# h of the last two batches as seven block products over both, behind all of the attention

## The chip, the cores and the metric

One core of a Trainium2 chip runs the whole program. The metric is the device time of one execution in microseconds. Five engines work side by side and wait for one another by semaphores: TensorE (PE, with its weight loads PEld), VectorE (DVE), ScalarE (ACT), GpSimd (POOL) and SyncE (SP, here a queue of transfers). Each engine takes its instructions strictly in the order in which the program lists them.

## The reference

Sigmoid attention over 8 batches, 12 heads, 448 positions, 64 values a head, and behind it a SiLU layer over all 3584 tokens:

```python
scores = scale * np.matmul(q, k.transpose(0, 1, 3, 2)) - np.log(S)
attn = 1.0 / (1.0 + np.exp(-scores))
attn_out = np.matmul(attn, v)
x = attn_out.transpose(0, 2, 1, 3).reshape(B * S, H * D)   # 3584 x 768
h = x @ w_in                                               # 768 x 2048
g = h * (1.0 / (1.0 + np.exp(-h)))
out = g @ w_out                                            # 2048 x 768
```

## The kernel before

All weights stay in SBUF as f16, w_in as 6 chunks of 128 rows (`w_in_sb`), w_out as 16 (`w_out_sb`). The order of every engine's work is written out by hand (`manual_schedule`).

**Attention** goes by g, a group of four heads of one batch: three for a batch, 24 in all. A unit (g, ch) is one of seven score tiles of a group. `scores` issues four matmuls of 64 x 64 for it, whose result stands in two PSUM banks, and a Sigmoid on ScalarE (L207) into `attnT`. A unit uses a pair of banks of the pool `ps_sc` (two pairs, 4 banks); the first unit of a burst of three takes two single banks of the pool `ps_1` (4 banks) instead, with two Sigmoids. The Sigmoid of the third unit of a burst is put off (L180) until other work of ScalarE's has been issued. `values` (L218) multiplies the seven tiles of a group by v in two single banks (`pav`); two scalings on VectorE (L243) write them into `xT` of the batch, and this releases the next loads.

**h** of a batch is 16 units (`h_unit`, L255), each 6 matmuls of 448 columns into one single bank `ph` (L262), a Sigmoid on ScalarE (`tsig`, L274) and a product on VectorE (L276) into `gTr`. `gTr` holds two batches side by side: 16 blocks of 128 features by 896 tokens.

**The output** goes by sets (`out_set`, L319) of two blocks of 128 tokens: seven products of 8 matmuls of 384 columns (`po`, L338; Strassen's scheme in Winograd's form), with four sums of gTr on VectorE (`S`, lines 350 to 360), eight scaled adds into `osb` (L346) and one copy `m1` on ScalarE (L353). A pair of batches m has three sets; its seventh token block is kept (`kept`, L412) until the next pair has one too, and the two make a fourth set. Four sums of w_out are made once (`w_sums`).

**Order.** `all_moe` is a generator that yields after each matmul of h and output: h of batch 2m, for m > 0 the first set, h of batch 2m + 1, the other sets. The main loop takes bursts of two or three score units (`burst`), the values of a group that is complete, the rows of a later one (copied on VectorE, transposed by a DMA on SP's queue, `dma_transpose`), and then a stretch of that stream (`stretch`), as long as the pace of the batch says. Loads of q, k and v are issued on GpSimd's queue, three or four groups ahead.

Of the kernel before, what the change touches and what calls it, by code (L numbers as in the profile page):

```python
# [17 lines left out]
def kernel(  # L18
# [9 lines left out]
    nc = tc.nc  # L28
# [116 lines left out]
    def pe_transpose(g, pieces=(("k", 0, 4), ("k", 4, NCH), ("q", 0, 4), ("q", 4, NCH))):  # L145
        if ("k", g) not in qkT:
            new_qkT(g)
        for name, c0, c1, *copy in pieces:
# [12 lines left out]
                dst[:, c0 * P : c1 * P], ptr[:, : (c1 - c0) * P]  # L161
            )

    def dma_transpose(g, name, copy):
        if ("k", g) not in qkT:
            new_qkT(g)
        rows = p3.tile([P, NCH, 2, D], F16, tag=f"{name}r", name=f"{name}r")
        copy(rows, flat[name, g].rearrange("p j c d -> p c j d"))  # L168
        nc.sync.dma_start_transpose(
            out=qkT[name, g], in_=rows.rearrange("p c j d -> p (c j d)")  # L170
        )

    attnT = {}

    late = []

# [5 lines left out]
    def scores(g, ch, banks=None, put_off=False):  # L182


        attnT[g, ch] = p12.tile([P, 2, S], F16, tag="attnT", name="attnT")
        if banks is None:
            psc = ps_sc.tile([P, 2, 512], F32, tag="pssc", name="psc")
            banks = [psc[:, j] for j in range(2)]
            parts = [(attnT[g, ch], psc[:, :, :S])]
        else:  # L190
            parts = [(attnT[g, ch][:, j], banks[j][:, :S]) for j in range(2)]
        for half in range(2):
            own = slice(half * HP, (half + 1) * HP)
            for j in range(2):
                rows = slice(j * D, (j + 1) * D)
                nc.tensor.matmul(  # L196
                    banks[j][own, :S],
                    qkT["k", g][rows, ch, own],
                    qkT["q", g][rows, :, own],
                    start=True,  # L200
                    stop=True,
                )
        if put_off:
            late.extend(parts)
            return
        for to, psc in parts:
            nc.scalar.activation(to, psc, AF.Sigmoid, bias=bias_s, scale=QKSCALE)  # L207
# [10 lines left out]
    def values(g, end=NCH):  # L218
        b, iq = divmod(g, NQ)
        if b not in xT:  # L220
            assert b < 2 or b - 2 in h_done
            xT[b] = p2.tile([P, NPAIR, S], F16, tag="xT", name="xT")
        pav, done_rounds = part_of.pop(g, None) or (
            [ps_1.tile([P, 512], F32, tag="ps1", name="pav") for _ in range(2)],
            0,
        )
        for ch in range(done_rounds, end):
            at = attnT.pop((g, ch))
            for half in range(2):
                own = slice(half * HP, (half + 1) * HP)  # L230
                for j in range(2):
                    nc.tensor.matmul(  # L232
                        pav[half][j * D : (j + 1) * D, :S],
                        flat["v", g][own, j, ch, :],
                        at[own, j, :],
                        start=(ch == 0),
                        stop=(ch == NCH - 1),
                    )
        if end < NCH:
            part_of[g] = pav, end  # L240
            return
        for half in range(2):
            nc.vector.tensor_scalar_mul(xT[b][:, half * NQ + iq, :], pav[half][:, :S], SX)  # L243
        if iq == NQ - 1:
            ready.add(b)

# [69 lines left out]
    def row_blocks(m, g):  # L316
        return [rows_of[2 * m + u // NCH, u % NCH] for u in (2 * g, 2 * g + 1)]

    def out_set(a1, rows1, a2, rows2, last=False):  # L319
        nonlocal hold, weight  # L320
        weight = SET_WEIGHT
        lo, hi = slice(0, NHC), slice(NHC, NFC)
        osb = [p4.tile([P, DMODEL], F32, tag="osb", name="osb") for _ in range(2)]
        c11, c12 = (osb[0][:, nh * NO2 : (nh + 1) * NO2] for nh in range(2))
        c21, c22 = (osb[1][:, nh * NO2 : (nh + 1) * NO2] for nh in range(2))
        m1 = p2.tile([P, NO2], F32, tag="m1", name="m1")
        sg = [cpool.tile([P, NHC, P], F16, tag=f"S{i}", name=f"S{i}") for i in range(1, 5)]

        def store(rows, o, cols, engines):
            for at, (row, eng) in enumerate(zip(rows, engines)):  # L330
                eng.dma_start(row[:, cols], o[at * HP : (at + 1) * HP, cols])

        left, right, whole = slice(0, NO2), slice(NO2, DMODEL), slice(0, DMODEL)

        def product(a, w):
            po = ps_1.tile([P, 512], F32, tag="ps1", name="po")
            for fc in range(NHC):
                nc.tensor.matmul(  # L338
                    po[:, :NO2], a[:, fc, :], w[:, fc, :], start=(fc == 0), stop=(fc == NHC - 1)
                )  # L340
                if fc < NHC - 1:
                    yield 163
            return po[:, :NO2]

        def plus(o, po, x, sign=ISX):
            nc.vector.scalar_tensor_tensor(  # L346
                out=o, in0=po, scalar=sign, in1=x, op0=ALU.mult, op1=ALU.add
            )

        nc.vector.tensor_sub(sg[2], a1[:, lo], a2[:, lo])  # L350
        nc.vector.tensor_add(sg[0], a2[:, lo], a2[:, hi])
        po = yield from product(a1[:, lo], wq[0][0])
        nc.scalar.activation(m1, po, AF.Copy, scale=ISX)  # L353
        late_sigmoid()
        nc.vector.tensor_sub(sg[1], sg[0], a1[:, lo])
        hold = False
        yield 163
        po = yield from product(a1[:, hi], wq[1][0])
        plus(c11, po, m1)
        nc.vector.tensor_sub(sg[3], a1[:, hi], sg[1])  # L360
        if last:
            store(rows1, osb[0], left, (nc.sync, nc.sync))
        yield 163
        po = yield from product(sg[2], tw[3])
        plus(c22, po, m1)
        yield 163
        po = yield from product(sg[1], tw[2])
        plus(c22, po, c22)
        plus(c12, po, m1)
        yield 163  # L370
        po = yield from product(a2[:, hi], tw[4])
        plus(c21, po, c22, -ISX)
# [12 lines left out]
        yield 163  # L385


    by_h1 = {3: 6, 6: 7, 9: 8}
    early = [h_unit(0, fc) for fc in range(2)]
    sums = w_sums()  # L390

    def moe_h(b):
        for fc in range(NFC):
            yield from early[fc] if b == 0 and fc < 2 else h_unit(b, fc)
            if b == 1:
                if fc >= 2:
                    next(sums)
                if fc in by_h1:
                    for name in ("k", "q"):
                        dma_transpose(by_h1[fc], name, act_copy)  # L400
                    if by_h1[fc] == 8:

                        nc.gpsimd.tensor_copy(gate, qkT["q", 8][:1, 0, :1])
                        for to in (10, 11, 12):
                            load("kq", to)

    def moe_set(m, g):
        step = out_set(block(g), row_blocks(m, g), block(g + 1), row_blocks(m, g + 1))
        for i, ns in enumerate(step):
            if m % 2 == 0 and g == 2 and i % 8 == 4 and i < 32:  # L410
                fcs = slice(i // 8 * 4, i // 8 * 4 + 4)
                nc.scalar.activation(kept[:, fcs], block(NCH - 1)[:, fcs], AF.Copy)  # L412
            if m == 0 and g == 0 and i in (10, 14):
                next(sums)
            if m == 0 and g == 0 and i in (24, 40):
                dma_transpose(9, "k" if i == 24 else "q", nc.vector.tensor_copy)
                if i == 40:
                    load("kq", 13)
            yield ns

    def all_moe():
        for m in range(B // 2):
            yield from moe_h(2 * m)
            if m > 0:
                yield from moe_set(m, 0)
            yield from moe_h(2 * m + 1)
            if m == 0:
                yield from moe_set(m, 0)
            yield from moe_set(m, 2)
            yield from moe_set(m, 4)  # L430
            if m % 2 == 1:
                g = NCH - 1
                yield from out_set(
                    kept, row_blocks(m - 1, g), block(g), row_blocks(m, g), m == B // 2 - 1
                )

    later = []
# [144 lines left out]
            do(*what)  # L582

    TILES = {2: 3, 3: 2, 4: 3, 5: 3, 6: 3, 7: 3}
    paces = {1: 1600, 2: 2400, 3: 2500, 4: 3400, 5: 3200, 6: 3000, 7: 2800}
    def burst(n, tiles):

        new = units[n : n + (tiles if not waiting else 2)]
# [56 lines left out]
```

## Time and profile before

| | us |
|---|---|
| median of 3 runs | 378.05 (377.73 to 378.10) |
| the profiled execution | 377.84 |
| its span, first to last instruction | 376.0 |
| TensorE busy in the span | 367.9 |
| last score matmul begins a burst at | 317.99 |
| h of batch 7, 96 matmuls in a row | 326.42 to 344.58 |
| last 168 output matmuls | 344.58 to 371.9 |

| stretch, us | PE | DVE | ACT | POOL | DMA share |
|---|---|---|---|---|---|
| 29 to 52 | 22.19 | 11.56 | 19.36 | 11.63 | 1.27 |
| 52 to 152 | 99.99 | 70.23 | 72.28 | 21.77 | 1.09 |
| 152 to 322 | 169.93 | 103.93 | 116.54 | 12.81 | 0.53 |
| 326 to 345 | 19.00 | 10.28 | 8.54 | 0.00 | 0.15 |
| 345 to 376 | 26.88 | 20.76 | 1.64 | 0.00 | 0.29 |

A share of busy time is an average over stages that differ. Matmuls are pipelined and the profile models their ends, so a busy TensorE need not be at its peak. The granted clock is 1.00 throughout. In the list of groups, each line has the line of the kernel, the engine, what is written and read, how often, the busy time and the mean of one, and the idle time ahead of it with the engine that ended it.

### The profile page before, as it was taken

To read this page: it belongs to the slowest core of one execution; us is meant where nothing else is said; L and a number is where in the kernel's file an instruction comes from. 1 tells how busy PE (TensorE), PEld (TensorE's weight loads), DVE (VectorE), ACT (ScalarE), POOL (GpSimd) and SP (SyncE) were. 2 spreads that over 40 slices of the span, in tenths; PEclk is the share of its full clock that TensorE was granted. 3 is DMA by queue.
4 is the path that set the end of the run, shared out by engine and by line. 5 is a ranking of instruction groups with operands and counts; after the bars stand their busy time and mean duration, and the time that the engine had idled before them with its cause. 6 is when DMAs were issued, how large, how long until landed. Compare 5 with 4: busy or idle time off the path is not lost.

```text
span 376.0 us, 7623 instructions
## 1 busy us (share of the span) xinstructions
PE 367.9 (98%) x3081; PEld 189.2 (50%) x3081; DVE 233.9 (62%) x417; ACT 243.2 (65%) x355; POOL 66.1 (18%) x99
## 2 busy tenths in 40 slices
PE   7999999999999999999999999999999999999995
PEld 3554445555554455455555545544555445555663
DVE  2664447997666466548676547645675457556773
ACT  5998886778766866676557676677866685243000
POOL 8566432053211002102120200000010000000000
PEclk9999999999999999999999999999999999999999
DMA  8999999959999909909499834546072300200333
GB/s 131 200 204 201 205 203 204 180 89 142 215 178 182 217 2 111 189 32 118 71 160 161 145 92 75 51 108 75 0 149 36 85 2 2 54 30 2 83 86 84
DMA packets 65698, 42.79 MB, mean 114 GB/s; under 512 B 36096, under 2 KB 62208, under 8 KB 65664
## 3 DMA queue, kind: packets, MB, share of 16 engines
q0 software_dynamic: 27072, 22.58, 42.5%
q1 hardware_dynamic: 38240, 19.44, 29.0%
q8 instruction: 24, 0.39, 0.4%
q10 hardware_dynamic: 352, 0.30, 0.2%
q14 instruction: 10, 0.08, 0.1%
HBM read 45.61 MB, written 11.01 MB: 151 GB/s over the span
## 4 chain that ended last, share of the span: by engine, by line
PE 91%; DMA 3%; ACT 2%; POOL 2%; issue 1%; DVE 0%; POOLq 0%; ACTq 0%
PE ph L262 38%; PE po L338 34%; PE psc L196 9%; PE pav L232 8%; DMA qf<-in_q_dram 3%; ACT attnT L207 1%; POOL kf L82 1%; POOL vf L82 1%; PE ptrq L153 0%; POOL qf L82 0%; ACT tsig L274 0%; DVE gTr L276 0%; ACT attnT L180 0%; PE ptrk L153 0%; DVE osb L346 0%
## 5 line engine op out<-in xcount | busy, mean ns | idle before, releaser
L207 ACT ACTIVATE attnT<-psc,bias_s 128x896 f16<-128x896 f32 (+1 forms) x168 | 138.5, 894 | 45.1 <-PE psc L196 44.9
L262 PE MATMUL ph<-xT,w_in_sb 128*128 128x448 f16 x768 | 151.2, 353 | 0.0
L276 DVE TENSOR_TENSOR gTr<-ph,tsig 128x448 f16<-128x448 f32 x128 | 78.3, 623 | 71.4 <-ACT tsig L274 70.9
L262 PEld LDWEIGHTS <-w_in_sb 128*128 128x128 f16 x768 | 72.8, 98 | 74.0 <-issue 9.2
L274 ACT ACTIVATE tsig<-ph 128x448 f16<-128x448 f32 x128 | 68.3, 549 | 49.1 <-PE ph L262 48.2
L338 PEld LDWEIGHTS <-S 128*128 128x128 f16 x448 | 42.3, 98 | 33.5 <-issue 7.2
L346 DVE SCALAR_TENSOR_TENSOR osb<-po,osb 128x384 f32<-128x384 f32 x70 | 37.6, 554 | 22.2 <-PE po L338 21.9
L196 PE MATMUL psc<-qT,kT 64*64 64x448 f16 x672 | 49.1, 360 | 1.5 <-ACT qT L143 0.5
L243 DVE TENSOR_SCALAR xT<-pav 128x448 f16<-128x448 f32 x48 | 27.7, 620 | 28.9 <-PE pav L232 28.9
L82 POOL DMA_DIRECT2D vf<-in_v_dram x24 | 17.2, 718 | 161.0 <-PE pav L232 138.6
L338 PE MATMUL po<-T,S 128*128 128x384 f16 x224 | 40.6, 327 | 0.0
L338 PEld LDWEIGHTS <-gTr 128*128 128x128 f16 x304 | 28.7, 98 | 23.5 <-issue 5.4
L338 PE MATMUL po<-w_out_sb,S 128*128 128x384 f16 x224 | 39.9, 326 | 0.0
L232 PE MATMUL pav<-attnT,vf 64*64 64x448 f16 x672 | 38.1, 350 | 0.4 <-DVE gTr L276 0.4
L338 PE MATMUL po<-w_out_sb,gTr 128*128 128x384 f16 x192 | 34.9, 327 | 0.0
L196 PEld LDWEIGHTS <-kT 64*64 64x64 f16 x672 | 16.4, 105 | 28.3 <-issue 23.1
L232 PEld LDWEIGHTS <-vf 64*64 64x64 f16 x672 | 20.9, 107 | 12.6 <-issue 2.7
L346 DVE SCALAR_TENSOR_TENSOR osb<-po,m 128x384 f32<-128x384 f32 x42 | 23.2, 553 | 6.3 <-PE po L338 5.1
L180 ACT ACTIVATE attnT<-psc,bias_s 128x896 f16<-128x896 f32 x26 | 26.6, 1022 | 0.0
L353 ACT ACTIVATE m<-po 128x384 f32<-128x384 f32 x14 | 6.9, 495 | 23.7 <-PE po L338 23.7
L338 PE MATMUL po<-T,gTr 128*128 128x384 f16 x112 | 21.4, 326 | 0.0
L82 POOL DMA_DIRECT2D kf<-in_k_dram x25 | 18.0, 721 | 18.0 <-DVE kr L168 9.6
(43 smaller groups left out, 153.6 us busy)
## 6 DMA issues: line engine op xcount, KB each, us to landing
out_dram<-osb SPq DMA_DIRECT2D x54, 192.0 KB, 3.2
vf<-in_v_dram POOLq DMA_DIRECT2D x24, 224.0 KB, 6.1
kf<-in_k_dram POOLq DMA_DIRECT2D x23, 224.0 KB, 7.9
qf<-in_q_dram POOLq DMA_DIRECT2D x23, 224.0 KB, 8.1
w_in_sb<-in_moe_w_in_dram POOLq DMA_DIRECT2D x16, 192.0 KB, 8.3
w_out_sb<-in_moe_w_out_dram POOLq DMA_DIRECT2D x4, 768.0 KB, 15.7
kT<-kr SPq DMA_TRANSPOSE x18, 7.3
qT<-qr SPq DMA_TRANSPOSE x18, 6.7
```

Source lines behind the costliest of these rows:

```text
L82: nc.gpsimd.dma_start(flat[name, g][:, :, c0:c1].rearrange("p i c d -> p i (c d)"), rows_in(name, g)[:, :, c0 * D : c1 * D],)
L180: nc.scalar.activation(to, psc, AF.Sigmoid, bias=bias_s, scale=QKSCALE)
L196: nc.tensor.matmul(banks[j][own, :S], qkT["k", g][rows, ch, own], qkT["q", g][rows, :, own], start=True, stop=True,)
L207: nc.scalar.activation(to, psc, AF.Sigmoid, bias=bias_s, scale=QKSCALE)
L232: nc.tensor.matmul(pav[half][j * D : (j + 1) * D, :S], flat["v", g][own, j, ch, :], at[own, j, :], start=(ch == 0), stop=(ch == NCH - 1),)
L243: nc.vector.tensor_scalar_mul(xT[b][:, half * NQ + iq, :], pav[half][:, :S], SX)
L262: nc.tensor.matmul(ph[:, :S], w_in_sb[:, cc, fc * P : (fc + 1) * P], xT[b][:, cc, :], start=(at == 0), stop=(at == NCC - 1),)
L274: nc.scalar.activation(tsig, ph[:, :S], AF.Sigmoid, bias=0.0, scale=ISX)
L276: nc.vector.tensor_mul(gTr[:, fc, (b % 2) * S : (b % 2) * S + S], ph[:, :S], tsig)
L338: nc.tensor.matmul(po[:, :NO2], a[:, fc, :], w[:, fc, :], start=(fc == 0), stop=(fc == NHC - 1))
L346: nc.vector.scalar_tensor_tensor(out=o, in0=po, scalar=sign, in1=x, op0=ALU.mult, op1=ALU.add)
L353: nc.scalar.activation(m1, po, AF.Copy, scale=ISX)
```

## The change

For the last two batches (6, "even", and 7, "odd") h is no longer made batch by batch. w_in is cut into four quadrants (two halves of the features by two halves of the 768 inputs), the two batches' xT into four blocks, and seven products replace eight. `h_pair` goes by f, the 8 pairs of feature blocks f and f + 8. For each f it makes seven products of 3 matmuls: `first(f)` makes products one and two, `group(f)` makes six, seven and five, three and four. Products one, two and six take single banks; seven and five share one pair of `ps_sc` banks, three and four the other. `first(0)` and `first(1)` run ahead of groups 0 and 1; from f = 2 on, `first(f)` runs just ahead of `group(f)`.

The seven results are combined by adds on VectorE into f32 tiles `mid` (in the buffers of `attnT`), by copies on ScalarE and ten adds on GpSimd; SiLU is then one function on ScalarE (`AF.Silu`) straight into `gTr`, in place of the Sigmoid and the product on VectorE. The scale 1/64 goes into it, so the last sets use a scale of 1 (`scale_of`), and the kept block is rescaled when it is copied.

Sums of the operands are made ahead: 16 of w_in (four kinds for each quarter t, one kind in place, the others in buffers of the attention that are free by then; `next_w_in_sum`, called in the h of batch 5 and in the sets of m = 2), and 12 of xT (`x_sums`, four behind the values of each group of batch 7). The first set of m = 2 moves behind the h of batch 5. The paces of batches 4 to 7 go from 3400, 3200, 3000, 2800 to 2800, 2500, 2350, 2300, so that the score units end while the sets of m = 2 still run.

The core of the diff:

```diff
@@ values @@
+        if b == B - 1:
+            x_sums(iq)
@@ out_set @@
-    def out_set(a1, rows1, a2, rows2, last=False):
+    def out_set(a1, rows1, a2, rows2, scale=ISX, last=False):
-        nc.scalar.activation(m1, po, AF.Copy, scale=ISX)
+        nc.scalar.activation(m1, po, AF.Copy, scale=scale)
+    def w_in_sum(i, t):
+        a11, a12, a21, a22 = (w_in_part(r, c, t) for r in range(2) for c in range(2))
...
+        if i == 1:
+            nc.vector.tensor_add(a21, a21, a22)
+        elif i == 2:
+            nc.vector.tensor_sub(ws[2, t], a21, a11)
+        elif i == 3:
+            nc.vector.tensor_sub(ws[3, t], a11, a21)
+        else:
+            nc.vector.tensor_sub(ws[4, t], a12, ws[2, t])
+    def x_sums(iq):
...
+        b11, b12, b21, b22 = even[:, iq], odd[:, iq], even[:, NH + iq], odd[:, NH + iq]
+        nc.vector.tensor_sub(xs[1, iq], b12, b11)
+        nc.vector.tensor_sub(b12, b22, b12)
+        nc.vector.tensor_sub(xs[2, iq], b22, xs[1, iq])
+        nc.vector.tensor_sub(xs[4, iq], b21, xs[2, iq])
+        xs[3, iq] = b12
+    def h_pair():
...
+        def silu(fc, b, h):
+            nc.scalar.activation(
+                gTr[:, fc, b % 2 * S : (b % 2 + 1) * S], h, AF.Silu, bias=0.0, scale=ISX
+            )
...
+        def first(f):
+            one, m1, c11 = single(), middle(), middle()
+            yield from product(one, f, quadrant(0, 0), x_part(0, even))
+            act_copy(m1, one)
+            while put_off:
+                silu(*put_off.pop(0))
+            yield 189
+            two = single()
+            yield from product(two, f, quadrant(0, 1), x_part(1, even))
+            nc.vector.tensor_add(c11, two, m1)
+            silu(f, even, c11)
+            yield 189
+            return m1
+        def group(f, m1):
+            u2, u3, u4, c22, c21 = (middle() for _ in range(5))
+            six = single()
+            yield from product(six, f, w_sum(2), x_sum(2))
+            nc.vector.tensor_add(u2, six, m1)
+            yield 189
+            seven, five = pair()
+            yield from product(seven, f, w_sum(3), x_sum(3))
+            yield 189
+            yield from product(five, f, w_sum(1), x_sum(1))
+            nc.vector.tensor_add(u3, seven, u2)
+            nc.vector.tensor_add(c22, five, u3)
+            nc.vector.tensor_add(u4, five, u2)
+            silu(NHC + f, odd, c22)
+            yield 189
+            three, four = pair()
+            yield from product(three, f, w_sum(4), x_part(1, odd))
+            yield 189
+            yield from product(four, f, quadrant(1, 1), x_sum(4))
+            if f == NHC - 1:
+                nc.vector.tensor_add(c21, four, u3)
+                silu(NHC + f, even, c21)
+                nc.vector.tensor_add(u4, three, u4)
+                silu(f, odd, u4)
+            else:
+                act_copy(c21, four)
+                if f % 2 == 0:
+                    nc.vector.tensor_add(u4, three, u4)
+                else:
+                    act_copy(u2, three)
+                nc.gpsimd.tensor_add(c21, c21, u3)
+                if f % 2 == 1:
+                    nc.gpsimd.tensor_add(u4, u2, u4)
+                put_off.extend(((f, odd, u4), (NHC + f, even, c21))[:: 1 if f % 2 == 0 else -1])
+            yield 189
@@ moe_h, moe_set @@
+            if b == B - 3:
+                units_done = fc + 1
+                next_w_in_sum()
...
+            if m == B // 2 - 2 and i % 8 == 4:
+                next_w_in_sum()
@@ all_moe @@
-            yield from moe_h(2 * m)
-            if m > 0:
-                yield from moe_set(m, 0)
-            yield from moe_h(2 * m + 1)
-            if m == 0:
+            if m == B // 2 - 1:
+                yield from h_pair()
+            else:
+                yield from moe_h(2 * m)
+                if m == 1:
+                    yield from moe_set(m, 0)
+                yield from moe_h(2 * m + 1)
+            if m != 1:
                 yield from moe_set(m, 0)
@@ paces @@
-    paces = {1: 1600, 2: 2400, 3: 2500, 4: 3400, 5: 3200, 6: 3000, 7: 2800}
+    paces = {1: 1600, 2: 2400, 3: 2500, 4: 2800, 5: 2500, 6: 2350, 7: 2300}
```

More of the change, by code (lines that the diff above doesn't have):

```diff
@@ L162, in pe_transpose @@
             )
+    in_rows = set()
     def dma_transpose(g, name, copy):
@@ L166, in dma_transpose @@
             new_qkT(g)
+        in_rows.add((name, g))
         rows = p3.tile([P, NCH, 2, D], F16, tag=f"{name}r", name=f"{name}r")
@@ L173 @@
     attnT = {}
+    scored = 0
     late = []
@@ L182, in scores @@
     def scores(g, ch, banks=None, put_off=False):
+        nonlocal scored
+        scored = g + (ch == NCH - 1)
         attnT[g, ch] = p12.tile([P, 2, S], F16, tag="attnT", name="attnT")
@@ L343, in product, with plus @@
             return po[:, :NO2]
-        def plus(o, po, x, sign=ISX):
+        def plus(o, po, x, sign=scale):
             nc.vector.scalar_tensor_tensor(
@@ L371, in out_set @@
         po = yield from product(a2[:, hi], tw[4])
-        plus(c21, po, c22, -ISX)
+        plus(c21, po, c22, -scale)
         yield 163
@@ L385, in out_set, with w_in_part @@
         yield 163
+    NH = NCC // 2
+    ws = {}
+    def w_in_part(r, c, t):
+        at = r * DFF // 2 + 2 * t * P
+        return w_in_sb[:, c * NH : (c + 1) * NH, at : at + 2 * P]
+    def w_in_sum(i, t):
+        a11, a12, a21, a22 = (w_in_part(r, c, t) for r in range(2) for c in range(2))
+        if i == 1:
+            ws[1, t] = a21
+        elif i == 4:
+            kT = p4.tile([P, NCH, P], F16, tag="kT", name="w4")
+            ws[4, t] = kT.rearrange("p c t -> p (c t)")
+        else:
+            tag = "kf" if i == 3 else "qf"
+            f = p4.tile([P, 2, NCH, D], F16, tag=tag, name=f"w{i}")
+            ws[i, t] = f.rearrange("p i c d -> p (i c d)")
+        if i > 1:
+            ws[i, t] = ws[i, t][:, : NH * 2 * P].rearrange("p (c f) -> p c f", c=NH)
+        if i == 1:
+            nc.vector.tensor_add(a21, a21, a22)
[5 more added lines that the diff above has]
+            nc.vector.tensor_sub(ws[4, t], a12, ws[2, t])
@@ new lines, with next_w_in_sum @@
+    w_in_sums = [(i, t) for t in range(4) for i in (3, 1, 2, 4)]
+    units_done = 0
+    def next_w_in_sum():
+        blocked = set()
+        for i, t in w_in_sums:
+            g = NQB - 4 + t
+            if (
+                units_done > NHC + 2 * t + 1
+                if i == 1
+                else scored > g
+                if i == 4
+                else ("k" if i == 3 else "q", g) in in_rows
+            ) and t not in blocked:
+                w_in_sums.remove((i, t))
+                w_in_sum(i, t)
+                return
+            blocked.add(t)
@@ new lines @@
+    xs = {}
+    def x_sums(iq):
+        even, odd = xT[B - 2], xT[B - 1]
+        if not xs:
+            rows = [
+                p3.tile([P, NCH, 2, D], F16, tag=f"{name}r", name=f"x{name}").rearrange(
+                    "p c j d -> p (c j d)"
+                )
+                for name in "kkkqq"
+            ]
+            for i, (at, end) in {
+                1: (rows[0], rows[1][:, :S]),
+                2: (rows[2], rows[1][:, S:]),
+                4: (rows[3], rows[4][:, :S]),
+            }.items():
+                for c in range(NH):
+                    xs[i, c] = at[:, c * S : (c + 1) * S] if c < 2 else end
+        b11, b12, b21, b22 = even[:, iq], odd[:, iq], even[:, NH + iq], odd[:, NH + iq]
[4 more added lines that the diff above has]
+        xs[3, iq] = b12
@@ new lines, in h_pair, with middle, product, quadrant @@
+    def h_pair():
+        even, odd = B - 2, B - 1
+        put_off = []
+        def middle():
+            return p12.tile([P, S], F32, tag="attnT", name="mid")
+        def product(o, f, a, x):
+            for c in range(NH):
+                nc.tensor.matmul(o, a(f, c), x(c), start=(c == 0), stop=(c == NH - 1))
+                if c < NH - 1:
+                    yield 189
+        def quadrant(r, c):
+            at = r * DFF // 2
+            return lambda f, i: w_in_sb[:, c * NH + i, at + f * P : at + (f + 1) * P]
+        def w_sum(i):
+            return lambda f, c: ws[i, f // 2][:, c, f % 2 * P : (f % 2 + 1) * P]
+        def x_part(r, b):
+            return lambda c: xT[b][:, r * NH + c, :]
+        def x_sum(i):
+            return lambda c: xs[i, c]
+        def silu(fc, b, h):
+            nc.scalar.activation(
+                gTr[:, fc, b % 2 * S : (b % 2 + 1) * S], h, AF.Silu, bias=0.0, scale=ISX
+            )
+        def single():
+            return ps_1.tile([P, 512], F32, tag="ps1", name="ph")[:, :S]
+        def pair():
+            both = ps_sc.tile([P, 2, 512], F32, tag="pssc", name="ph2")
+            return both[:, 0, :S], both[:, 1, :S]
+        def first(f):
+            assert even in ready and not w_in_sums
+            one, m1, c11 = single(), middle(), middle()
[11 more added lines that the diff above has]
+        def group(f, m1):
+            assert odd in ready
+            u2, u3, u4, c22, c21 = (middle() for _ in range(5))
[31 more added lines that the diff above has]
+                put_off.extend(((f, odd, u4), (NHC + f, even, c21))[:: 1 if f % 2 == 0 else -1])
+            yield 189
+        m1s = []
+        for f in range(2):
+            m1s.append((yield from first(f)))
+        for f in range(NHC):
+            m1 = m1s[f] if f < 2 else (yield from first(f))
+            yield from group(f, m1)
+        h_done.update((even, odd))
@@ L392, in moe_h @@
     def moe_h(b):
+        nonlocal units_done
         for fc in range(NFC):
             yield from early[fc] if b == 0 and fc < 2 else h_unit(b, fc)
+            if b == B - 3:
+                units_done = fc + 1
+                next_w_in_sum()
             if b == 1:
@@ L405, in moe_h, with scale_of @@
                             load("kq", to)
+    def scale_of(m):
+        return 1.0 if m == B // 2 - 1 else ISX
     def moe_set(m, g):
-        step = out_set(block(g), row_blocks(m, g), block(g + 1), row_blocks(m, g + 1))
+        step = out_set(
+            block(g), row_blocks(m, g), block(g + 1), row_blocks(m, g + 1), scale_of(m)
+        )
         for i, ns in enumerate(step):
@@ L411, in moe_set @@
                 fcs = slice(i // 8 * 4, i // 8 * 4 + 4)
-                nc.scalar.activation(kept[:, fcs], block(NCH - 1)[:, fcs], AF.Copy)
+                nc.scalar.activation(
+                    kept[:, fcs],
+                    block(NCH - 1)[:, fcs],
+                    AF.Copy,
+                    scale=scale_of(m) / scale_of(m + 1),
+                )
+            if m == B // 2 - 2 and i % 8 == 4:
+                next_w_in_sum()
             if m == 0 and g == 0 and i in (10, 14):
@@ L422, in all_moe @@
         for m in range(B // 2):
-            yield from moe_h(2 * m)
-            if m > 0:
-                yield from moe_set(m, 0)
-            yield from moe_h(2 * m + 1)
-            if m == 0:
+            if m == B // 2 - 1:
+                yield from h_pair()
+            else:
+                yield from moe_h(2 * m)
[3 more added lines that the diff above has]
+            if m != 1:
                 yield from moe_set(m, 0)
@@ L433, in all_moe @@
                 yield from out_set(
-                    kept, row_blocks(m - 1, g), block(g), row_blocks(m, g), m == B // 2 - 1
+                    kept,
+                    row_blocks(m - 1, g),
+                    block(g),
+                    row_blocks(m, g),
+                    scale_of(m),
+                    m == B // 2 - 1,
                 )
```

## The prediction

> **What bounds the kernel now.** I read the page's busy shares first, then the busy times by stretch, then the chain that ended last, then the timeline at the end.
>
> ```profile
> PE 367.9 (98%) x3081; PEld 189.2 (50%) x3081; DVE 233.9 (62%) x417; ACT 243.2 (65%) x355; POOL 66.1 (18%) x99
> ...
> PE 91%; DMA 3%; ACT 2%; POOL 2%; issue 1%; DVE 0%; POOLq 0%; ACTq 0%
> PE ph L262 38%; PE po L338 34%; PE psc L196 9%; PE pav L232 8%; DMA qf<-in_q_dram 3%; ACT attnT L207 1%; POOL kf L82 1%; POOL vf L82 1%; PE ptrq L153 0%; POOL qf L82 0%; ACT tsig L274 0%; DVE gTr L276 0%; ACT attnT L180 0%; PE ptrk L153 0%; DVE osb L346 0%
> ```
> ```profile
> 152.00:322.00 170.00, 169.93 (x1385) 87.35 (x1381) 103.93 (x183) 116.54 (x177) 12.81 (x18) 1.00 0.53 84
> ...
> 326.00:345.00 19.00, 19.00 (x103) 9.91 (x102) 10.28 (x17) 8.54 (x16) 0.00 (x0) 1.00 0.15 42
> ```
>
> The columns of the second fence are PE, PEld, DVE, ACT and POOL busy, the granted clock, the DMA share and GB/s. TensorE is the chain for 91% of the span, at full clock. A busy PE in this profile need not be PE at its peak, so I checked with counts. The chain gives the price of each kind: 96 matmuls of h in 18.16 us (0.189 each), 168 of the output in 27.31 (0.163 each), 28 of the values in 1.32, three units of scores in 0.69 (0.23 each). From 152 to 318, counts times these prices leave only 0.10 to 0.16 us per burst of scores, but for one place:
>
> ```profile
> 267.13 0.49 ACT m L353
> 267.62 1.95 ACT attnT L207 x3
> 269.57 0.52 ACT kept L412
> 270.09 0.91 ACT attnT L180
> 271.00 0.04 issue
> 271.04 0.38 PE psc L196 x4
> ```
>
> Here the second score unit of a burst waits for the bank pair that the put-off sigmoid of the burst before (L180) still reads; it costs about 0.4 us. The reader is to see that a burst of three units keeps ScalarE for at least 0.4 + 1.95 + 0.95 = 3.3 us, so a burst must be followed by that much TensorE work.
>
> **The change, part by part.**
>
> *Fewer matmuls.* h of batches 6 and 7 is 2 x 16 x 6 = 192 matmuls; seven products of 3 for each of 8 pairs of blocks are 168. The order of the built program shows 744 matmuls of h in place of 768. 24 x 0.189 = **-4.54 us**. Nothing else leaves TensorE.
>
> *All attention earlier.* From unit 84 on, the stretches between bursts hold 288 matmuls of h and 303 of the output in place of 384 and 370: TensorE's work there falls from 167.2 to 138.2 us by the prices above. ScalarE's, at 1.0 us a unit, 0.55 per h unit (L274) and 0.5 per m (L353), falls from about 121 to 112, so its share goes from 73% to 81%. In the h of batch 5 a burst of three is followed by 26 matmuls: TensorE 0.7 + 4.9 + 0.1 = 5.7, ScalarE 3.1 + 4.33 x 0.52 = 5.4. It fits, and the next burst, with values, has slack (ScalarE 3.5 of 5.1). Of the output sets of m = 2, the tightest bursts have 13 and 16 matmuls behind them. With 13 the next burst begins at 2.9 and its second unit at 3.15, while the put-off sigmoid ends at 3.3 to 3.4: 0.25. With 16 after a burst that had a kept copy (0.65) ahead of its put-off sigmoid, the shift passes on and the second unit waits about 0.5. Together 0 to 1.2; I take **+0.5**.
>
> *Sums on VectorE.* 16 of w_in (128 x 768 f16: L308's row, 0.549) are 8.8 us; 12 of x (448 f16) go by the slope between 768 (0.549) and 1024 (0.685) elements to 0.38 each, 1.6 us per group of four since each needs the one before. VectorE had 103.9 busy of 170; less 16 gTr (0.62) and 1.2 sets (7.2 each), plus 8.8 and two x groups, it has about 97 of 140. Idle time covers them, and the score bursts wait on the xT scalings, which stand ahead of the x sums. Where cover is gone is the last pav: its second bank waits for c11 of the set's second product. From the end of the pav before, VectorE has two xT (1.2), four x sums (1.6), one osb (0.5), three S (1.9), a w_in sum (0.5) and c11 (0.55): 6.3. TensorE has 11 + 17 output matmuls and a burst: 1.8 + 0.8 + 2.8 = 5.4. I take **+0.8** (0 to 1.1). The third x group is covered by the 31 output matmuls and two `first` units behind it (5.0 + 2.3 us against 2.8).
>
> *Banks of h.* Each group's first pair (products seven and five) is freed by u3, c22 and u4 on VectorE. In steady state five more products (2.83 us) pass before it is wanted again; three adds at 0.62 (L276's row, same size out of PSUM) need about 2.0. Between groups 0 and 1 only three products (1.70) pass, and the Silu table load stands in ScalarE's queue between the two m1 copies. The only load in the trace took 1.28 us (L481). With h starting at 0: m1 of block 0 is copied by 1.3, the load ends at 2.55, Silu of c11 at 3.1, the second m1 copy at 3.55, then VectorE's c11 4.2, u2 4.75, u3 5.4, c22 6.05, u4 6.6. The pair is wanted at 5.67: **+0.9** (0 without the load's delay, 1.0).
>
> The Trainium skill ("ScalarE: Activation LUTs", Terms) puts a table load at about 2.7 us; the trace has 1.28 and decides. By the page the last term would be an estimated 2.4 and the sum 1.4 higher.
>
> *Per pair of groups* TensorE has 42 x 0.189 = 7.94, ScalarE 13 operations at a pitch of about 0.47 to 0.5 (6.3), VectorE 11 adds (6.4): all fit. But one circle runs through two engines: m1 copy, then c11, u2, u3, c22 (2.5, the dependent ones at full length), Silu of c22 (0.59), copies of c21 and the next m1 (0.93) = 4.0, and 4.5 in an odd group with u2's copy: 8.5 against 7.94. The excess of 0.54 per two groups is first taken from slack; walking it on, seven waits 0.3 at group 5 and 0.5 at group 7. Bounds 0 and 1.6 (three times 0.54): **+0.4**.
>
> *End of h.* The first output set's second product needs Silu of the last c21. With ScalarE idle that is 0.2 + 0.62 + 0.04 + 0.55 + 0.05 = 1.46 after the last h matmul, against 8 x 0.163 = 1.30 of the first product: 0.16. With the circle's lateness (Silu of c22 ends 1.75 after the last h matmul, then c21's) it is 1.55. Between: **+0.9**. Before, this seam had none: the h of batch 7 ran into a set whose blocks it finished early.
>
> *GpSimd* gets 10 adds of 448 f32. No two-input operation of it is in the trace. Memsets of 128 x 1 and 128 x 128 (0.096, 0.224) give 1.0 ns an element, the affine select (one read, 0.289) 1.5; two reads at 0.5 each make 2.0 ns, 0.1 + 0.9 = 1.0 us. Bounds 0.62 (VectorE's add) and 2.0 (twice). At 1.0 it sets nothing. Its loads and SP's transposes keep their places: loads land after 6 to 8 us and are used three and four heads later, over 30 us even now. SP's stores of the last sets only stand later, with 27 us of output behind the first.
>
> **Sum** against the profiled execution: 376.0 - 4.54 + 0.5 + 0.8 + 0.9 + 0.4 + 0.9 = 375.0 of span. Its own time was 377.84 (1.84 around the span) and the median is 378.05, 0.2 more. So 375.0 + 1.84 + 0.2 = **377.0 us**, 1.0 less than before.
>
> **Rivals.**
>
> 1. *All cover holds* (fast): the five stalls at their low bounds, 0 + 0 + 0 + 0 + 0.16, give 378.05 - 4.4 = 373.7. For it: TensorE had no idle in 170 us of like bursts. Against: the wait at 271 shows such seams cost something when work behind a burst is short.
> 2. *GpSimd's adds set the end* (slower): in odd groups two adds follow one another and ScalarE's queue waits for the second. Copy of c21, two adds, three Silus, copies, adds and Silu of the next group make 6.0 + 2g for an add of g, against 7.94; from g = 1.24 it overtakes the 8.5 circle. At g = 1.5, 9.0 - 7.94 = 1.06 three times is 3.2 in place of 0.4, and the end seam grows to 1.3: 377.0 + 2.8 + 0.4 = 380.2. Against: the slope above.
> 3. *The first GpSimd add alone is long*. The group-1 adds queue behind it; each us beyond about 3.5 delays ScalarE, and so the pair, by one. From 5.3 the change is slower; at 6, 377.0 + 2.5 = 379.5. Against: the first memset and select in the trace show no such gap. The Trainium skill ("GPSIMD Engine Reference", 2.1 Instruction dispatch) says that the first call to a freshly loaded kernel pays some 6 us that show as no instruction; no run here yet shows it for an add.
> 4. *Attention becomes ScalarE's* (slower): bursts at 5.4 of 5.7 us leave 0.3. If the order of Sigmoids and bank waits eats it, six such bursts at 0.4 are 2.4, and the sets go to 1.2: 377.0 + 2.4 + 0.7 = 380.1. Against: bursts at 89% (297 to 304) ran without a stall.
>
> **How the numbers follow.** Forecast 0.45 (own range 375.9 to 378.2), rival 1 0.17, 2 0.15, 3 0.08, 4 0.15. About 0.2%, 0.76 us, is what can be told from no change, so faster means below 377.3. Two thirds of the forecast's chance lies there, with all of rival 1: 0.47. Slower (above 378.8) are rivals 2 to 4 but for a sliver: 0.37. The rest, 0.16, is the same. The range leaves out the fast half of rival 1 and the slow ends of 2 to 4: **374.3 to 380.4**.
>
> **What would show it.** 744 h matmuls; the stretch of 168 last ones longer than 31.8 us by about 1.3; product seven of group 1 waiting on u4; the last pav waiting on VectorE near 0.8; the second product of the first last set waiting on a Silu; score units waiting on L184's Sigmoid in the sets of m = 2. Wrong it would be if waits of TensorE add up to over 5 us or under 2, or if GpSimd's add is over 1.24.

## The result

The change makes the kernel a little slower: 379.58 us (379.01 to 379.91, 6 runs) against 378.08 (377.72 to 378.42, 6 runs), a ratio of 1.0038 (95% interval 1.0025 to 1.0051). The forecast was 377.0, faster by 1.0; the time fell inside the range of 374.3 to 380.4, on the other side of no change.

The profiled execution took 379.65, its span 377.9. First the busy shares and the chain of waits on the page of the changed kernel:

```profile
PE 366.9 (97%) x3057; PEld 188.1 (50%) x3057; DVE 251.7 (67%) x459; ACT 251.9 (67%) x374; POOL 77.3 (20%) x109
...
PE 80%; ACT 8%; DVE 8%; issue 3%; DVEq 0%; ACTq 0%
```

TensorE has 24 matmuls fewer, which at 0.189 each are 4.54 us, yet its busy time falls by only 1.0, and it is the chain for only 80% of the span where it was 91%: 8% each now run through ScalarE and VectorE. Next the list of what TensorE waited for (total, times, longest); the lines left out stand in the list of the kernel before as well:

```profile
PE ph L483 <- DVE mid L543: 1.7, 3, 1.0
...
PE po L346 <- ACT gTr L501: 0.4, 1, 0.4
...
PE pav L238 <- DVE osb L354: 0.3, 1, 0.3
PE psc L202 <- ACT attnT L184: 0.2, 1, 0.2
PE po L346 <- DVE S L358: 0.2, 1, 0.2
```

L483 is the line of all the new products, L543 the add that makes u4. These lines show where to look, not how much is lost: short waits are not listed, and the busy time that fell by 1.0 in place of 4.54 shows that some of the loss counts as busy. So I measured stage by stage, as length less count times price (0.189, 0.163, 1.32 and 0.23, as in the prediction). The busy times by stretch (PE, PEld, DVE, ACT and POOL busy, granted clock, DMA share, GB/s) of the attention, of the seven products and of what follows them:

```profile
152.00:291.00 139.00, 138.79 (x1201) 70.47 (x1197) 91.51 (x169) 104.04 (x156) 12.84 (x18) 1.00 0.57 95
301.50:336.20 34.70, 32.92 (x170) 16.39 (x169) 24.53 (x44) 24.43 (x48) 11.24 (x10) 1.00 0.09 23
```

In the second stretch TensorE is idle for 1.8 of 34.7 us, at a granted clock of 1.00.

| what TensorE lost or gained, us | predicted | measured | from |
|---|---|---|---|
| 24 fewer matmuls of h | -4.54 | -4.54 | 744 h matmuls (576 and 168) |
| attention closer together | +0.5 | +1.13 | excess over counts from the burst at 147.27 to the last one at 290.79: 5.32; before, from 146.55 to 317.99: 4.19 |
| last value product | +0.8 | +0.87 | its end at 296.44; by counts 295.57 |
| bank pair of groups 0 and 1 | +0.9 | +1.18 | from product six to seven of group 1: 306.59 to 308.34, by counts 0.57 |
| circle of ScalarE and VectorE | +0.4 | +1.71 | the seven of groups 2 to 7 come 4.06, 4.13, 4.22, 4.48, 4.15 and 4.49 after those of the group before, by counts 3.97 |
| end of h | +0.9 | +0.91 | from the last product of h to product three of the set: 336.17 to 339.68, by counts 2.60 |
| sum | -1.04 | +1.26 | |

The row of the last value product is its whole excess over the counts. The same instructions of the kernel before, from its last burst at 317.99 to 323.49, have 0.23 of it already, so 0.64 is new and the sum by that is 1.03.

The spans of the two profiled executions differ by 1.9. The first score burst of batch 2 began at 77.54 before and at 78.27 after, though both kernels list the same work up to there; 1.9 less that 0.73 is 1.17, close to both sums.

The bank pair, in the timeline of the changed kernel (start, length, engine, line, operation, in brackets the idle time and what ended it):

```profile
302.31 0.54 ACT L143 ACTIVATE mid<-ph 128x448 f32<-128x448 f32 x1 [8.08 <-PE ph L483]
302.88 1.28 ACT L501 ACT_TABLE_LOAD   x1
...
304.17 0.58 ACT L501 ACTIVATE gTr<-mid 128x448 f16<-128x448 f32 x1
...
304.65 0.52 ACT L143 ACTIVATE mid<-ph 128x448 f32<-128x448 f32 x1
...
306.59 0.73 PE L483 MATMUL ph<-xk,w 128*128 128x448 f16 x3
...
307.67 0.61 DVE L543 TENSOR_TENSOR mid<-ph,mid 128x448 f32<-128x448 f32 x1
...
308.34 0.73 PE L483 MATMUL ph<-xT,w 128*128 128x448 f16 x3 [1.01 <-DVE mid L543]
```

The table load stands between the two copies of m1, as walked in the prediction, and product seven of group 1 starts within 0.06 us of the end of u4. The Trainium skill ("ScalarE: Activation LUTs", Terms) has about 2.7 us for a load; here it took 1.28 and the Silu behind it began at once, so the trace differs and decides.

The circle, one turn of two groups:

```profile
325.17 0.96 ACT L143 ACTIVATE mid<-ph 128x448 f32<-128x448 f32 x2
325.23 0.73 PE L483 MATMUL ph<-xT,w 128*128 128x448 f16 x3 [0.35 <-DVE mid L543]
...
326.26 0.61 DVE L523 TENSOR_TENSOR mid<-ph,mid 128x448 f32<-128x448 f32 x1
...
328.18 0.62 DVE L542 TENSOR_TENSOR mid<-ph,mid 128x448 f32<-128x448 f32 x1
...
328.83 0.58 ACT L501 ACTIVATE gTr<-mid 128x448 f16<-128x448 f32 x1 [0.85 <-DVE mid L542]
329.32 1.39 ACT L143 ACTIVATE mid<-ph 128x448 f32<-128x448 f32 x3
...
333.80 0.96 ACT L143 ACTIVATE mid<-ph 128x448 f32<-128x448 f32 x2
333.87 0.73 PE L483 MATMUL ph<-xT,w 128*128 128x448 f16 x3 [0.35 <-DVE mid L543]
```

Read it as a ring: the copies at 325.17 release c11 (L523), a row of dependent adds on VectorE ends in c22 (L542), ScalarE stands idle 0.85 until it can make the Silu of c22, and only behind that Silu, in its queue, come the copies that release the next c11. From 325.17 to 333.80 one turn takes 8.63; TensorE's 42 matmuls need 7.94. GpSimd is not in it, but by a small margin. Its adds took 1.14 (7 and 3 of them), the first 1.13; ScalarE waits for the second of two in a row (Silu at 323.54), and the Silu of c22 two places behind (324.68) then comes only 0.1 later than ScalarE could have begun it.

And the attention, in the chain of waits of the changed kernel, at the output set behind the h of batch 5:

```profile
262.29 0.49 ACT m L361
262.78 1.95 ACT attnT L213 x3
264.73 0.91 ACT attnT L184
265.63 0.04 issue
265.68 0.38 PE psc L202 x4
```

It is the picture that the kernel before had at 269.57 to 271.04: the second score unit of a burst waits for the bank pair that the put-off Sigmoid (L184) still reads. The burst at 184.05, in a set of m = 1, loses as much in another way, as the timeline of VectorE ahead of it shows:

```profile
182.85 0.61 DVE L171 COPY kr<-kf 128x896 f16<-128x896 f16 x1
183.37 0.55 DVE L354 SCALAR_TENSOR_TENSOR osb<-po,osb 128x384 f32<-128x384 f32 x1
183.84 0.55 DVE L354 SCALAR_TENSOR_TENSOR osb<-po,m 128x384 f32<-128x384 f32 x1
```

The second matmul of that burst starts at 184.44, 0.05 after the last of these adds, which frees its single bank; a copy of rows for a transpose (L171) stands ahead of the two adds. ScalarE was idle for 2.67 at this place.

### The profile page after: what moved, and what is told of

It reads as the page before. It is cut to its first block, busy times and chain, and to the rows that moved or that the text cites. A ratio compares the mean times of both kernels' runs of the same rounds, so it can differ in the third digit from the quotient of the medians.

```text
span 377.9 us, 7681 instructions
## 1 busy us (share of the span) xinstructions
PE 366.9 (97%) x3057; PEld 188.1 (50%) x3057; DVE 251.7 (67%) x459; ACT 251.9 (67%) x374; POOL 77.3 (20%) x109
## 4 chain that ended last, share of the span: by engine, by line
PE 80%; ACT 8%; DVE 8%; issue 3%; DVEq 0%; ACTq 0%
PE po L346 32%; PE ph L270 28%; PE psc L202 9%; PE pav L238 8%; ACT attnT L213 5%; ACT mid L143 2%; DVE mid L541 1%; DVE mid L542 1%; DVE mid L535 1%; PE pw L140 1%; DVE mid L523 1%; PE ptrq L153 1%; DVE osb L354 0%; DVE mid L558 0%; ACT tsig L282 0%
## 5 line engine op out<-in xcount | busy, mean ns | idle before, releaser
L270 PE MATMUL ph<-xT,w_in_sb 128*128 128x448 f16 x576 | 114.4, 353 | 0.0
L284 DVE TENSOR_TENSOR gTr<-ph,tsig 128x448 f16<-128x448 f32 x96 | 58.4, 621 | 51.7 <-ACT tsig L282 51.1
L270 PEld LDWEIGHTS <-w_in_sb 128*128 128x128 f16 x576 | 54.1, 98 | 56.5 <-issue 9.0
L282 ACT ACTIVATE tsig<-ph 128x448 f16<-128x448 f32 x96 | 50.7, 551 | 24.7 <-PE ph L270 24.3
L346 PEld LDWEIGHTS <-S 128*128 128x128 f16 x448 | 42.1, 98 | 34.5 <-issue 7.5
L202 PE MATMUL psc<-qT,kT 64*64 64x448 f16 x672 | 49.9, 360 | 1.6 <-ACT attnT L213 0.5
L346 PE MATMUL po<-T,S 128*128 128x384 f16 x224 | 40.6, 327 | 0.2 <-DVE S L358 0.2
L346 PEld LDWEIGHTS <-gTr 128*128 128x128 f16 x304 | 28.7, 98 | 23.4 <-issue 4.5
L346 PE MATMUL po<-w_out_sb,S 128*128 128x384 f16 x224 | 40.3, 327 | 0.0
L346 PE MATMUL po<-w_out_sb,gTr 128*128 128x384 f16 x192 | 34.9, 327 | 0.4 <-ACT gTr L501 0.4
L184 ACT ACTIVATE attnT<-psc,bias_s 128x896 f16<-128x896 f32 x26 | 26.5, 1021 | 0.0
L501 ACT ACTIVATE gTr<-mid 128x448 f16<-128x448 f32 x32 | 17.5, 575 | 10.7 <-DVE mid L542 6.5
```

The source lines that it names most:

```text
L202: nc.tensor.matmul(banks[j][own, :S], qkT["k", g][rows, ch, own], qkT["q", g][rows, :, own], start=True, stop=True,)
L270: nc.tensor.matmul(ph[:, :S], w_in_sb[:, cc, fc * P : (fc + 1) * P], xT[b][:, cc, :], start=(at == 0), stop=(at == NCC - 1),)
L282: nc.scalar.activation(tsig, ph[:, :S], AF.Sigmoid, bias=0.0, scale=ISX)
L284: nc.vector.tensor_mul(gTr[:, fc, (b % 2) * S : (b % 2) * S + S], ph[:, :S], tsig)
L346: nc.tensor.matmul(po[:, :NO2], a[:, fc, :], w[:, fc, :], start=(fc == 0), stop=(fc == NHC - 1))
L501: nc.scalar.activation(gTr[:, fc, b % 2 * S : (b % 2 + 1) * S], h, AF.Silu, bias=0.0, scale=ISX)
```

## The experiments

All are measured against the kernel before on the same chip (its medians were 378.3 to 378.6), so ratios are what compares. The line numbers of an experiment's profile can be a few off those of the changed kernel.

**The Silu of c22 put off** behind the next copy of m1:

```diff
-            silu(NHC + f, odd, c22)
+            if f == NHC - 1:
+                silu(NHC + f, odd, c22)
+            else:
+                put_off.append((NHC + f, odd, c22))
```

> One edit to the changed kernel: the Silu of c22 goes into the put-off list (but for the last group), so ScalarE copies c21 and the next m1 without waiting for VectorE's c22. Theory (the circle m1 copy, c11, u2, u3, c22, Silu, c21 copy, m1 copy runs at 8.6 us per two groups against TensorE's 7.94): the waits of product seven at groups 3 to 7 go, 1.5 to 1.9 us in all; h_pair takes about 32.9 us in place of 34.7, the seam behind it shrinks by some 0.5; time 377.3 to 378.1. Rival (VectorE's adds or the bank pairs themselves are too slow): the waits stay, time within 0.4 of the changed kernel's 379.6. GpSimd as the next limit: waits of ScalarE for its adds grow and half of the gain stays out, 378.6.

377.11 us (376.8 to 377.44), ratio 0.9972 (0.9962 to 0.9982). One Silu of each group (but the last) moved in one queue turns the change from slower to faster. The timeline of this kernel, ScalarE and TensorE at the end of the h:

```profile
328.25 2.08 ACT L501 ACTIVATE gTr<-mid 128x448 f16<-128x448 f32 x4
...
330.31 1.05 ACT L143 ACTIVATE mid<-ph 128x448 f32<-128x448 f32 x2
...
331.75 0.73 PE L483 MATMUL ph<-xT,w 128*128 128x448 f16 x3
...
336.96 2.80 PE L346 MATMUL po<-T,S 128*128 128x384 f16 x16 [0.17 <-DVE S L358]
```

Product seven of the last group (331.75) follows without a wait, ScalarE makes four Silus in one row, and the products take 32.96 us (301.06 to 334.02): 31.78 and the 1.18 of the bank pair. Of the 0.91 at the end of h, 0.3 is left. So the circle is shown, with what its lateness did to the seam.

**The table load ahead**, by a Silu of one column behind the last Sigmoid, in time that ScalarE has to spare:

```diff
+        nc.scalar.activation(warm, bias_s, AF.Silu, bias=0.0, scale=1.0)
         for g in waiting:
             values(g)
```

> One edit to the changed kernel: a one-column Silu right behind the last Sigmoid, so that the table load of 1.28 us falls in 8 us in which ScalarE is idle. Theory (the wait of 1.0 us of product seven in group 1 comes from the load that stands between the two m1 copies): that wait goes to 0.1 or less, time 0.7 to 1.2 lower, 378.4 to 378.9. Rival (only three products pass between the two uses of the pair, and three adds are too slow for that by themselves): the wait stays at 0.5 or more, time 379.2 or above. If the circle takes the gain back, the wait goes but h_pair ends less than 0.5 earlier.

378.87 us, ratio 1.0013 (1.0004 to 1.0022). In the timeline of this kernel:

```profile
305.64 0.73 PE L483 MATMUL ph<-xk,w 128*128 128x448 f16 x3
...
306.76 0.73 PE L483 MATMUL ph<-xT,w 128*128 128x448 f16 x3 [0.39 <-DVE mid L543]
```

From six to seven it is now 1.12 instead of 1.75: the load was 0.6 of the 1.18, and three products between the uses of one pair of banks cost 0.55 by themselves. The products took 34.07 (300.53 to 334.60), 0.61 less than in the changed kernel. From there on the sevens follow at 4.07, 4.13, 4.22, 4.49, 4.15 and 4.48, the distances of the changed kernel: the circle's loss is the same, whether group 1's seven comes 0.6 late or not.

**The last sum of w_in behind the last value product:**

```diff
-            if m == B // 2 - 2 and i % 8 == 4:
+            if m == B // 2 - 2 and i % 8 == 4 and not (g == 4 and i < 28):
                 next_w_in_sum()
```

> One edit to the changed kernel: the last sum of w_in (0.55 us on VectorE) is made behind the last pav in place of ahead of the add c11 that frees pav's second bank. Theory (VectorE is late there): the wait of pav for its second bank falls from about 0.8 to 0.3, nothing else moves, time 0.4 to 0.6 lower, 379.0 to 379.2. Rival (the bank waits for something else, or the sum is then missed later): no change or a new wait at product three of group 0.

378.91 us, ratio 1.0015 (1.0006 to 1.0024). The last value product, of the changed kernel and then of this one:

```profile
293.92 0.55 DVE L427 TENSOR_TENSOR w<-w_in_sb,w 128x768 f16<-128x768 f16 x1
294.35 0.38 PE L238 MATMUL pav<-attnT,vf 64*64 64x448 f16 x2
...
294.99 1.51 PE L238 MATMUL pav<-attnT,vf 64*64 64x448 f16 x26 [0.27 <-DVE osb L354]
```
```profile
294.19 1.69 PE L238 MATMUL pav<-attnT,vf 64*64 64x448 f16 x28
295.81 1.31 PE L346 MATMUL po<-T,S 128*128 128x384 f16 x7
```

In the changed kernel a sum of w_in (L427) stands in VectorE's queue ahead of the add of osb that frees the second bank, and the product breaks after two matmuls. Without it the 28 run in one piece. From the first of them to the next output matmul it is 1.62 in place of 2.09: 0.47 of the 0.87 was this one sum.

**Plain h, the earlier attention kept:** the two batches' h in 192 matmuls, the order and the paces of the change. The sums of w_in and x and the scale of 1 are taken back too, in lines left out here.

```diff
-                yield from h_pair()
+                yield from moe_h(2 * m)
+                yield from moe_h(2 * m + 1)
```

> The seven products are undone and the rest of the change kept: batches 6 and 7 get plain h units, one batch behind the other, with no sums of w_in and x, while the attention still ends ahead and the shorter paces stay. Theory (the earlier attention costs about 1.1 us of TensorE in bursts whose second score unit waits for a put-off Sigmoid and in the h of batch 5): TensorE's h is back at 768 matmuls, no waits in h, time about 379.2 (378.08 + 1.1), and the seven products with their sums are worth +0.4. Rival (the earlier attention costs nothing): 378.1, and all of the loss is inside the seven products. Rival (it costs more, the sums being innocent): over 380.

379.54 us, ratio 1.0032 (1.0020 to 1.0043). The attention's excess is 5.31 here and 5.32 in the changed kernel, alike at the two largest bursts (0.49 at 183.62 and 0.54 at 264.67; 0.49 at 184.05 and 0.55 at 265.09); in h of batch 5 it lies at other bursts, with the same sum of 0.41 above the usual. So the earlier attention alone costs the 1.2 us by which this kernel is slower, the sums on VectorE cost the bursts nothing in all, and the seven products as written bring nothing: their 4.54 goes into 0.64 + 1.18 + 1.71 + 0.91 = 4.44 of waits that this kernel lacks (its last value product has the 0.23 of the kernel before).

**The three edits together** (Silu of c22, table load, sum of w_in):

> The three edits that each gained are made together: Silu of c22 behind the next copy of m1, a one-column Silu behind the last Sigmoid, and no sum of w_in ahead of the last value product. Circle theory: the circle's 1.9 us and the seam's .6 go (as when the first was made alone, 377.1), the wait of group 1's seven goes from 1.01 to about .4 and this time nothing takes it back, since the circle has slack (-.6), and the value product runs unbroken (-.6). Time about 376.0 us (375.7 to 376.4), ratio about .994; the h of the last two batches takes about 32.3 us. Rival (the gains share one cover, as they did when the table load alone was moved): 376.9 to 377.2, with h at 32.9 or more.

376.09 us (376.02 to 376.28), ratio 0.9944 (0.9931 to 0.9956). The products take 32.33 (300.95 to 333.28): 31.78 and the short gap's 0.55. The gains add up, as the theory had it.

**The first products one group ahead**, so that five products pass between groups 0 and 1 too:

```diff
         for f in range(NHC):
-            m1 = m1s[f] if f < 2 else (yield from first(f))
-            yield from group(f, m1)
+            yield from group(f, m1s[f])
+            if f + 2 < NHC:
+                m1s.append((yield from first(f + 2)))
```

As written this leaves out part of the computation: no `first` follows group 6, so its three put-off Silus (1.7 us of ScalarE's time) are never made.

> As the run with the three edits, and the two first products of group f+2 pass right behind the seven of group f, so that five products (8 x .189 x 5 = 7.9 us less the pair itself) and not three lie between groups 0 and 1 too. If what is left of the wait of group 1's seven (about .4) is the short gap, it goes: 375.6 us, ratio .993, h at 31.8 to 32.0. Rival: VectorE and ScalarE now get c11 of group f+2 ahead of the last steps of group f's chain, a circle comes back and the waits of each group's seven with it: the same time as the run with the three edits or up to 1 us longer.

375.90 us, ratio 0.9931 (0.9919 to 0.9944), not to be told from the run before it; where the three Silus are lacking, at the end of h, it is no fair comparison (2.60 to product three there, 2.92 in the run before). The 7.9 us that was expected between two uses of the pair is a slip: five products of three matmuls are 2.83. The timeline of this kernel at its last two groups:

```profile
329.83 0.73 PE L483 MATMUL ph<-xk,w 128*128 128x448 f16 x3
331.11 0.73 PE L483 MATMUL ph<-xT,w 128*128 128x448 f16 x3 [0.54 <-DVE mid L543]
```

Neither theory: the wait of group 1 is gone and no circle came back, but there are eight pairs of first products, and with two ahead the pair lacking is that between groups 6 and 7. The gap was moved, not closed.

**The same with longer paces** (2850, 2600, 2450, 2450 for batches 4 to 7), with the same three Silus left out:

> As the run with five products between all groups, with paces of 2850, 2600, 2450 and 2450 for the last four attention batches in place of the change's: the attention then ends nearer to the h, with 10 output matmuls left behind the last value product instead of 31, and the tightest bursts have 17 or 18 matmuls between their score units instead of 13 to 16. If the attention stage's added 1.1 us is the short distance of bursts, .5 to .8 of it goes: about 375.0 us, ratio .991 to .992. Rival: with less behind the last value product the sums of x or w_in are late for the first of the seven, and a new wait there takes the gain: 375.6 or more.

375.91 us, ratio 0.9934 (0.9920 to 0.9947): the rival's outcome. The h began 1.1 us earlier (299.78 against 300.89) and took 1.06 longer: 0.45 more at its first four products, 0.14 at product six of group 1, and 1.01 instead of 0.54 ahead of the last seven.

**The first products directly ahead of every group**, the three edits kept:

```diff
-        m1s = []
-        for f in range(2):
-            m1s.append((yield from first(f)))
         for f in range(NHC):
-            m1 = m1s[f] if f < 2 else (yield from first(f))
+            m1 = yield from first(f)
             yield from group(f, m1)
```

> As the run with the three edits, but with the two first products of each group directly ahead of its seven, group 0 and 1 too; so five products lie between the paired products of all eight groups, and no short gap is left, where the version that ran one pair ahead moved it to the last two groups (.54 us there). Theory (the rest of the wait is the short gap of three products): the .39 goes and nothing takes it back: h of the last two batches at 31.8 to 31.95 us, 375.7 us, ratio .993. Rival: product six of group 0 comes 1.5 us earlier and finds the sums of x not made yet, or ScalarE is late for it: a new wait of .3 us or more ahead of group 0's seven products, 376.1 or more.

374.96 us (374.66 to 375.34), ratio 0.9913 (0.9898 to 0.9928). The chain on this kernel's page, and the stretch of its h products:

```profile
PE 91%; DMA 3%; ACT 2%; POOL 2%; issue 1%; DVE 0%; POOLq 0%; ACTq 0%
```
```profile
300.30:332.10 31.80, 31.80 (x170) 16.46 (x169) 25.81 (x46) 23.63 (x47) 11.23 (x10) 1.00 0.09 25
```

TensorE is busy for all of the 31.80 us; the 168 matmuls take 31.78, product three of the set follows 2.60 after them, and no wait of L483 or L346 is left in the list. The chain is again TensorE for 91%, as before the change. The time fell by 1.1, more than the 0.4 expected: 0.55 of the gap and 0.32 of the seam at the end of h (2.92 to 2.60) account for 0.87, and the rest is within the intervals.

**The same with the longer paces:**

> As the run with the first products directly ahead of each group, with the paces 2850, 2600, 2450 and 2450 of the last four attention batches. With the version that ran one pair ahead these paces brought the h of the last two batches 1.1 us forward, and the h then took 1.06 us longer: .45 at its first two products, behind output sums late on VectorE, .14 at group 6, and .47 more at the last short gap. Theory (the 1.1 us are the short distances of the bursts, the loss is of the seam): only the last short gap is gone here, so .4 to .5 are left over: 375.2 us, ratio .9915 to .9925. Rival: what ScalarE or VectorE must still do after the last value product sets the start of the h in any case; the sum stays as without the paces, 375.7 or more.

374.60 us (374.03 to 374.79), ratio 0.9898 (0.9881 to 0.9914), the fastest version. The attention's excess is 4.46 in place of 5.33, so the short distances of the bursts were 0.87 of the 1.13; 0.28 went to the first group's products one and two (1.42 us instead of 1.14). The intervals of these last two overlap, so what the paces bring by themselves rests on the traces more than on the times: from the first score burst of batch 2 to the end of the span, one execution of this kernel took 294.70 and one of the kernel before it 295.36.

## Why the prediction was wrong, by its own steps

The waits of TensorE that it priced at 3.5 us in all came to 5.80, over the 5 that it had named as a sign of being wrong; 1.31 of the excess is the circle, 0.63 the attention.

- *Fewer matmuls, -4.54*: right, and shown as a time. The version without stalls and the plain h have the same attention and paces; their ratios, 0.9913 and 1.0032, differ by 0.0119, which of 378.5 is 4.5 us.
- *All attention earlier, +0.5*: right in kind, too small at 1.13. The usual excess of a burst is 0.11, or 0.15 with values. In the sets of m = 2 the burst behind 13 matmuls (265.09) lost 0.39 above it, where 0.25 was walked, and the two at 283.45 and 286.92 lost 0.22 together, where 0.5 was. The kernel before had 0.26 of this kind. Two losses were not in the walk: 0.38 at 184.05, where a bank waits for VectorE, and 0.41 in h of batch 5, of which the prediction said "It fits", at three bursts (226.56, 243.24, 249.10); at the first and third a bank waits for a gTr product on VectorE (L284). The longer paces took most of it away.
- *Sums on VectorE, +0.8*: 0.87 by the counts, of which 0.23 was there before the change: 0.64 is what it cost. 0.47 was the one sum of w_in; what made the other 0.17 was not tried.
- *Banks of h, +0.9*: right in place and cause, 1.18 in size. The low bound of "0 without the load's delay" was wrong: with the load out of the way 0.55 stayed.
- *The circle, +0.4*: this is the step that failed most. The ring was named and its turn was estimated at 8.5; it is 8.63. What went wrong is the sentence that its excess "is first taken from slack", with the 0.3 and 0.5 at groups 5 and 7 then cut down to 0.4. Of three turns at an excess of 0.69, the first lost 0.25, the second 0.76 and the third 0.70: 1.71 in all, just over the upper bound of 1.6, with a slack of 0.4 where the walk had 0.8. My reading is that group 1's seven, which waits for u4 with the table load and without it, leaves TensorE level with VectorE, and that a waiting TensorE has no slack to give; no run started the ring without that wait, so this stays argued. The 1.3 of error is over half of the 2.3 between forecast and sum.
- *End of h, +0.9*: right in size (0.91). Of the place only half: the second product's first seven matmuls ran on, its last waited for a Silu (0.39), and then product three for S on VectorE (0.18). With the circle gone 0.3 was left, with all stalls gone nothing.
- *GpSimd*: right; 1.14 an add against the 1.0 taken, under the 1.24 of rival 2. ScalarE does wait for it in the changed kernel, 0.4 to 0.5 at a time, in odd groups; it still does, 0.4 at a time, in the version whose TensorE never stops in the h, so it costs the end nothing. In the changed kernel its path ends 0.1 ahead of the circle's, closer than the sum of rival 2 had it. Rival 3 falls: the first add took 1.13 and began 0.08 after the copy that it waited for. The rule of the Trainium skill ("GPSIMD Engine Reference", 2.1 Instruction dispatch) named there, some 6 us at the first call to a freshly loaded kernel, did not show; whether the add's code was freshly loaded, the trace does not tell.
- *Rival 4* (attention becomes ScalarE's) priced 3.6. The attention lost 1.13 in all, and only 0.61 of the waits (265.09, 283.45, 286.92) are behind a put-off Sigmoid.

## What to carry to other kernels

A ring that runs through two in-order engines has to be compared with the period of the loop like an engine's load, and its excess is paid nearly in full each turn as soon as the slack ahead of it is gone. Look first in such a ring for an instruction that nobody waits for soon, here a Silu that stood ahead of a copy: moving it one place was worth about 2.4 us. Where two uses of a buffer have less work between them at one point of a loop, check whether a reordering closes the gap or only moves it to the other end.

## What the runs showed of the hardware

- The ACT_TABLE_LOAD for Silu held ScalarE for 1.28 us, with the next Silu directly behind it.
- A GpSimd add of two 128 x 448 f32 tiles in SBUF took 1.13 to 1.15 us, the first as long as the others; two in a row start 1.09 apart (321.28 and 322.37). VectorE's took, with one operand in PSUM, 0.61 to 0.63.
- Adds of VectorE that do not need each other start 0.54 us apart (332.66 and 333.20), dependent ones 0.66 to 0.72 (u2 at 331.28, u3 at 332.00, c22 at 332.66), at a length of 0.62. A ring is to be summed with the latter.
- The first score burst of batch 2 began between 77.29 and 78.27 us in kernels that list the same work up to there. Two spans can differ by nearly 1 us for that alone; stages have to be compared by their own length.
